# Both layers of a mixture-of-depths block as seven block products, in sections of one attention group

## The chip, the cores and the metric

The kernel runs on one core of a Trainium2 chip. The time is the device time of one execution in microseconds; three runs are shown, and the median counts. A core has five engines that run beside each other, each through its own list of instructions in order: TensorE (PE, with its weight loads as PEld), VectorE (DVE), ScalarE (ACT), GpSimd (POOL) and SyncE (SP, which issues most transfers). They wait for each other by semaphores.

## The reference

Attention with normalized queries and keys on 8 batches of 12 heads, 448 tokens and 64 values per head, then a layer that works on 128 chosen tokens of each batch:

```python
q_n, k_n = (rmsnorm(q, g_q), rmsnorm(k, g_k))          # (8, 12, 448, 64)
scores = scale * np.matmul(q_n, k_n.transpose(0, 1, 3, 2))
attn = softmax(scores)
x = np.matmul(attn, v)                                 # -> (8, 448, 768)
...
scores = np.einsum('bsd,d->bs', x, w_gate)
out = x.copy()
for b in range(B):
    top_idx = np.argpartition(-scores[b], capacity)[:capacity]   # capacity 128
    xe = x[b, top_idx]
    h = np.maximum(xe @ w1, 0.0)                       # w1 768 x 1024: layer 1
    ye = h @ w2                                        # w2 1024 x 768: layer 2
    g = 1.0 / (1.0 + np.exp(-scores[b, top_idx]))
    out[b, top_idx] = x[b, top_idx] + g[:, None] * ye
```

All is in float32.

## The kernel before, in words

**Attention.** The heads of a batch are three groups of four; 24 groups in all, numbered n. A group has seven units u (64 keys each, for four heads). `scores(u)` multiplies keys by queries into two PSUM banks of the pool `ps_sc` (four banks, handed out in turn) and has ScalarE take two exponentials into a tile `p` (seven of them). `values(u)` multiplies by v and collects a group in two banks of `ps_av`. `add_probs` adds the `p` tiles on VectorE; in the first six groups the last two units of a group are left to TensorE. When a group has ended, `values_out` copies its result out of PSUM on ScalarE (two copies), `sum_keys` makes the softmax sums (`den_ps`), `invert_sums` transposes them and takes the reciprocal on VectorE, and two calls of `to_tokens` transpose the result (four transposes each) and multiply it by the reciprocal on VectorE (x out of `x_ps`). `gate` multiplies by `w_gate` (four products on VectorE). For a whole batch follow `store_x`, `spread`, `score_rows` (four transposes and a copy), `count` (the rank of each token by comparisons on VectorE), `annotate`, `select` (four indirect DMAs on POOL that write the chosen rows to DRAM), and `load_selected` (SP loads them as `xe`).

**Preparing later groups** is laid in slots: `at(slot, fn)` runs `fn` when the loop has reached unit `slot`. The loads of tokens, q, k, v stand 11 to 26 units ahead, then `squares` (ScalarE), `sum_squares` (VectorE and POOL), `rows_out`, `rows_in` (through DRAM), `scale_q` (VectorE). The weights are loaded in 14 parts from slot 16 on, every third slot.

**The two layers** are in `mixture(g)`, a generator whose pieces the loop takes one at a time. The batches are grouped 0, 1-2, 3-4, 5-6, 7. For all of them layer 1 is the plain product: the weights are the stationary operand, and 128 tokens (a single batch) or 256 (a pair) are the moving one; ScalarE takes the maximum with 0 out of PSUM. Layer 2 of a single batch is plain too, 384 columns of w2 at a time. Layer 2 of a pair takes seven block products instead of eight: the hidden tiles are cut in a 2 x 2 block matrix (rows are the two batches, columns the halves of the hidden width), w2 in four blocks, and sums and differences of blocks (s1 to s4 on VectorE) are multiplied by w2 blocks or mixed blocks. The mixed blocks (`mix`, a subtraction on VectorE of 128 x 768 elements) are made once, stored to DRAM (`store_mixed`), and loaded again through a ring of two buffers (`load_mixed`). Four of the seven products add up in one bank, `main`; the others use a `side` bank of `ps_sc`. `gated` multiplies by the gate and adds to `xe` on VectorE; `write` puts the rows out by an indirect DMA.

**The loop** runs in sections of four units: scores of two, values of two, again, and after that up to two pieces of `mixture` and tasks from a list (`tasks`, `opening`), whose place is worked out while the program is made (`ready`, `pieces`, `long_next`, `single`). Batch 0's pieces start as soon as its chosen rows are there.

Of the kernel before, what the change touches and what calls it, by code (L numbers as in the profile page):

```python
# [68 lines left out]
def fast(  # L69
# [24 lines left out]
    CP = 112  # L94
# [30 lines left out]
    spare = [False]  # L125

    def aux(shape, name):

        if PER * now[0] >= units:
            return ps_sc.tile(shape, F32, tag="sc", name=name)  # L130
        if spare[0]:
            return ps_moe.tile(shape, F32, tag="moe", name=name)
        return ps_aux.tile(shape, F32, tag="aux", name=name)
# [38 lines left out]
    w1 = const.tile([128, NDC, F], F32, name="w1")  # L172
    HF, HD = NFC // 2, DM // 2
    w2 = {b: const.tile([128, HF, HD], F32, name=f"w2_{b[0]}{b[1]}") for b in ((0, 0), (1, 0), (1, 1))}
    mixed = [dram_pool.tile([128, HF, HD], F32, name=f"mixed{i}", bufs=1) for i in range(4)]
# [22 lines left out]
    def load_w(part):  # L198
        if part < NDC:
            nc.sync.dma_start(  # L200
                out=w1[:, part], in_=moe_w1.rearrange("(c p) f -> p c f", p=128)[:, part]
            )
            return
        k, part = divmod(part - NDC, 2)
        load_block(((0, 0), (1, 0), (0, 1), (1, 1))[k], part)

    def in_ring(what):
        ring[what] = moe_pool.tile([128, HF, HD], F32, name="ring", bufs=2)
        return ring[what]

    def chunk(part):
        return slice(HF // 2 * part, HF // 2 * (part + 1))

    def load_block(b, part):
        dst = w2[b] if b in w2 else ring["B12"] if part else in_ring("B12")
        src = moe_w2.rearrange("(k f p) (h c) -> k h p f c", p=128, f=HF, c=HD)[b[0], b[1]]
        nc.sync.dma_start(out=dst[:, chunk(part)], in_=src[:, chunk(part)])

    def load_mixed(i, part):
        dst = ring[i] if part else in_ring(i)  # L220
        nc.sync.dma_start(out=dst[:, chunk(part)], in_=mixed[i][:, chunk(part)])

    def store_mixed(i, part):
        nc.sync.dma_start(out=mixed[i][:, chunk(part)], in_=ring[i][:, chunk(part)])

    def mix(i, part):

        if part == 0:
            if i == 1:
                ring[1] = ring["B12"]  # L230
            else:
                in_ring(i)
        a, b = {
            1: (ring.get("B12"), w2[0, 0]),
            3: (w2[1, 1], ring.get("B12")),
            2: (w2[1, 1], ring.get(1)),
            0: (w2[1, 0], ring.get(2)),
        }[i]
        f = chunk(part)
        nc.vector.tensor_tensor(out=ring[i][:, f], in0=a[:, f], in1=b[:, f], op=OP.subtract)  # L240
# [104 lines left out]
    def values(u):  # L345
        n, i = divmod(u, NI)
        if i == 0:
            avs[n] = [ps_av.tile([128, 512], F32, name="av") for _ in range(2)]
        for hh in (1, 0):
            for c in range(2):  # L350
                r = slice(D * c, D * (c + 1))
                nc.tensor.matmul(  # L352
                    out=avs[n][c][D * hh : D * (hh + 1), 0:S],
                    lhsT=get("v", n)[r, hh, i, :],
                    rhs=probs[u][r, hh],
                    start=(i == 0),
                    stop=(i == NI - 1),
                )
# [13 lines left out]
    def values_out(n):  # L372
        for c in (1, 0):
# [11 lines left out]
    def sum_keys(n):  # L385

        add_late()
        ps = aux([128, 512], "den_ps")
# [16 lines left out]
        dens[n] = den  # L405
        if n < n_groups - 1:

            q, place = now
            when = (q, place + 1) if place == 0 or long_next(q) else (q + 1, 0)
            tasks.insert(0, (when, lambda: invert_sums(n)))  # L410

    def invert_sums(n):
        den = dens.pop(n)
        shape = [128, 128]
        if now[1] == 0 and PER * now[0] < units:
            pool, tag = (ps_moe, "moe") if before_layers(now[0]) else (ps_sc, "sc")
            ps = pool.tile(shape, F32, tag=tag, name="denT_ps")
        else:
            ps = aux(shape, "denT_ps")
        nc.tensor.transpose(out=ps[:CP, :], in_=den, identity=ident)  # L420
# [3 lines left out]
            in_=ps[:CP].rearrange("p (t r) -> p t r", r=32)[:, :, 0:NJ].rearrange(  # L424
# [5 lines left out]
    def to_tokens(n, c):  # L430
# [4 lines left out]
        shape = [128, NJ, 128]  # L435
        if c == 1 and not (before_layers(now[0]) or spare[0] or now[1] == 1 and single(now[0])):
            ps = ps_sc.tile(shape, F32, tag="sc", name="x_ps")
        else:
            ps = aux(shape, "x_ps")
# [8 lines left out]
        )  # L448

# [39 lines left out]
    def score_rows(b):  # L489
        if before_layers(now[0]):  # L490
            ps = aux([128, 512], "row_ps")
        else:

            ps = ps_sc.tile([128, 512], F32, tag="sc", name="row_ps")
# [65 lines left out]
    groups = [(0,)] + [(b, b + 1) for b in range(1, B - 2, 2)]  # L560
    groups += [(b,) for b in range(1 + 2 * (len(groups) - 1), B)]
    group_of = {b: g for g, bs in enumerate(groups) for b in bs}

    def mixture(g):

        n, bs = CAP, groups[g]
        G = len(bs)
        wide = 128 * G
        xe = [xes.pop(b) for b in bs]
        last = bs[-1] == B - 1  # L570
        xeT = moe_pool.tile([128, NDC, 2, 128], F32, name="xeT")
        hT = moe_pool.tile([128, NFC, 2, 128], F32, name="hT")

        def bank():

            if PER * now[0] >= units:
                return ps_sc.tile([128, 512], F32, tag="sc", name="sc")
            return ps_moe.tile([128, 512], F32, tag="moe", name="moe_ps")

        half = NDC // 2  # L580
        rows = []

        parts_out = ((0, HD), (DM - 2 * HD // 3, DM), (HD, DM - 2 * HD // 3)) if last else ((0, DM),)

        def write(i, k):
            c0, c1 = parts_out[k]
# [7 lines left out]
        def gated(i, cols, ps):  # L594
            x = xe[i]
            nc.vector.scalar_tensor_tensor(  # L596
                out=x[:n, cols],
                in0=ps[:n, : cols.stop - cols.start],
                scalar=x[:n, DM : DM + 1],
                in1=x[:n, cols],  # L600
# [3 lines left out]

        for i, x in enumerate(xe):
            for a in range(2):
                ps = ps_sc.tile([128, 512], F32, tag="sc", name="xeT_ps") if a else bank()
                for d in range(half):
                    dc = half * a + d
# [6 lines left out]
                    out=xeT[:, half * a : half * (a + 1), i, :n],  # L616
                    in_=ps[:, : half * 128].rearrange("p (i t) -> p i t", t=128)[:, :, :n],
                )
                if a == 1:
                    row = moe_pool.tile([128, len(parts_out)], I32, name="row", bufs=4)  # L620
                    for k, (c0, c1) in enumerate(parts_out):
                        nc.vector.tensor_scalar(
                            out=row[:n, k : k + 1],
                            in0=x[:n, DM + 1 : DM + 2],
                            scalar1=float(DM // (c1 - c0)),
# [863 lines left out]
```

## Time and profile before

| | |
|---|---|
| runs shown | 514.47, 518.47, 518.48 us, median 518.47 |
| the profiled execution | 513.42 us |
| its span, first to last instruction | 511.7 us |
| TensorE (PE) busy | 491.6 us, 96% |
| VectorE (DVE) busy | 354.0 us, 69% |
| ScalarE (ACT) busy | 274.8 us, 54% |
| GpSimd (POOL) busy | 187.0 us, 37% |
| layer 1, matmuls in the trace | 288 of 256 columns, 192 of 128 columns |
| layer 2, matmuls in the trace | 168 in products of pairs (384 columns), 64 for single batches |
| moved by DMA | 105.82 MB |

Times are measured from the start of the span. A matmul of float32 is two instructions in the trace. Of a group of instructions the busy time is that in which at least one of them ran; matmuls overlap, so their pace is read from start to start. L and a number is the line of the kernel.

### The profile page before, as it was taken

The page shows a single profiled execution, that of the slowest core. Times are in us where ns is not written, and L with a number is a line of the kernel's source. Part 1 is how long each engine was busy: PE and PEld are TensorE (multiplying, and loading weights), DVE is VectorE, ACT ScalarE, POOL GpSimd, SP SyncE. Part 2 cuts the span into 40 slices and gives each one's busy share as a digit, 9 for nine tenths or more (in the row PEclk, how much of TensorE's full clock was granted, in tenths as well). Part 3 has the DMA queues.
Part 4 walks back from the last instruction along what each step waited for, and adds up shares of the span by engine and source line. Part 5 has one row for each costly group of instructions (what it writes and reads, how often), then busy time and mean ns, then how long its engine had stood idle before and what let it go on. Part 6 is the DMA issues. An engine that isn't in the chain of part 4 may idle for free. (4 is left out here: it accounts for less than half of the span.)

```text
span 511.7 us, 11121 instructions
## 1 busy us (share of the span) xinstructions
PE 491.6 (96%) x4429; PEld 279.4 (55%) x4429; DVE 354.0 (69%) x670; ACT 274.8 (54%) x507; POOL 187.0 (37%) x104
## 2 busy tenths in 40 slices
PE   5999999988999999999999999999999899999994
PEld 4544445435555444666654454665554454786683
DVE  4566898699866898996687886777567686623201
ACT  4787886866757466665454737654634536310000
POOL 4694548444524174427123085036220022020102
PEclk9999999999999999999999999999999999999998
DMA  8977889999964673899461989567423318232601
GB/s 294 387 247 257 271 272 365 326 296 319 283 204 129 214 248 121 283 323 331 134 201 26 350 280 302 190 191 207 136 72 88 110 38 260 89 109 58 221 3 36
DMA packets 49295, 105.82 MB, mean 207 GB/s; under 512 B 11571, under 2 KB 26420, under 8 KB 49234
## 3 DMA queue, kind: packets, MB, share of 16 engines
q1 hardware_dynamic: 45826, 98.70, 59.9%
q0 software_dynamic: 3264, 6.31, 3.7%
q8 instruction: 37, 0.61, 0.5%
q14 instruction: 24, 0.20, 0.1%
q10 hardware_dynamic: 144, 0.00, 0.0%
HBM read 84.37 MB, written 28.50 MB: 221 GB/s over the span
## 5 line engine op out<-in xcount | busy, mean ns | idle before, releaser
L337 ACT ACTIVATE p<-sc,rinv 128x448 f32<-128x448 f32 x336 | 186.0, 641 | 88.3 <-PE sc L328 74.3
L256 POOL TENSOR_TENSOR rinv<-ss,neg_half 128x14 f32<-128x14 f32 (+1 forms) x49 | 135.7, 2775 | 184.4 <-DVE ss L255 164.9
L328 PE MATMUL sc<-qT,kT 64*64 64x448 f32 x1344 | 152.7, 545 | 1.0 <-DVE qT L307 0.8
L352 PE MATMUL av<-p,v 64*64 64x448 f32 x1344 | 147.0, 537 | 0.0
L368 DVE TENSOR_TENSOR sum<-sum,p 128x896 f32<-128x896 f32 x107 | 116.5, 1089 | 8.1 <-ACT p L337 1.9
L352 PEld LDWEIGHTS av<-p,v 64*64 64x64 f32 x1344 | 57.6, 133 | 69.6 <-issue 62.3
L328 PEld LDWEIGHTS sc<-qT,kT 64*64 64x64 f32 x1344 | 52.5, 132 | 69.3 <-issue 43.8
L255 DVE TENSOR_REDUCE ss<-sq 128x14 f32<-128x910 f32 (+1 forms) x49 | 52.1, 1074 | 11.9 <-ACT sq L246 11.6
L639 PE MATMUL moe_ps<-xeT,w 128*128 128x256 f32 (+1 forms) x288 | 56.1, 347 | 0.0
L539 POOL DMA_INDIRECT selected<-x,rank x32 | 35.8, 1118 | 47.7 <-DVE x L531 39.7
L639 PEld LDWEIGHTS moe_ps<-xeT,w 128*128 128x128 f32 x288 | 46.2, 191 | 6.8 <-issue 2.6
L246 ACT ACTIVATE sq<-tok 128x896 f32<-128x896 f32 (+1 forms) x49 | 45.9, 949 | 5.9 <-DMA tok<-in_tok_dram 5.6
L443 DVE TENSOR_TENSOR x<-x_ps,rden 112x512 f32<-112x512 f32 x48 | 32.5, 687 | 20.8 <-PE x_ps L441 18.3
L467 DVE SCALAR_TENSOR_TENSOR prod<-x,wg 112x256 f32<-112x256 f32 x96 | 40.6, 423 | 2.9
L587 POOL DMA_INDIRECT out_dram<-xe,row x10 | 10.5, 1052 | 85.7 <-DVE xe L596 67.9
L639 PE MATMUL sc<-xeT,w 128*128 128x256 f32 (+1 forms) x192 | 32.2, 328 | 0.3 <-ACT xeT L615 0.3
L441 PE MATMUL x_ps<-ident,xT 128*112 128x128 f32 x192 | 28.8, 276 | 2.0 <-DVE x L443 2.0
L639 PEld LDWEIGHTS sc<-xeT,w 128*128 128x128 f32 x192 | 28.8, 191 | 2.8 <-ACT xeT L615 0.5
L287 DVE SCALAR_TENSOR_TENSOR qT<-qT,gg,bc 128x896 f32<-128x896 f32 x22 | 25.3, 1149 | 4.4 <-DMA bc<-rows 4.4
L512 DVE SCALAR_TENSOR_TENSOR cmp<-score_rows,gate,earlier 112x448 f32<-112x448 f32 x32 | 21.9, 684 | 9.1 <-ACT score_rows L502 8.1
L441 PEld LDWEIGHTS x_ps<-ident,xT 128*112 128x112 f32 x192 | 21.8, 134 | 10.3 <-issue 4.5
L368 DVE TENSOR_TENSOR sum<-p 128x896 f32<-128x896 f32 x24 | 25.9, 1078 | 1.8 <-ACT p L337 1.8
(87 smaller groups left out, 331.9 us busy)
## 6 DMA issues: line engine op xcount, KB each, us to landing
tok<-in_tok_dram SPq DMA_DIRECT2D x48, 448.0 KB, 6.6
qT<-in_qT_dram SPq DMA_DIRECT2D x24, 448.0 KB, 6.6
kT<-in_kT_dram SPq DMA_DIRECT2D x24, 448.0 KB, 7.1
v<-in_vp_dram SPq DMA_DIRECT2D x24, 448.0 KB, 7.6
out_dram<-x SPq DMA_DIRECT2D x8, 1344.0 KB, 9.0
bc<-rows SPq DMA_DIRECT2D x44, 224.0 KB, 6.4
ring<-mixed SPq DMA_DIRECT2D x22, 384.0 KB, 5.3
xe<-selected SPq DMA_DIRECT2D x8, 385.0 KB, 3.7
```

Source lines behind the costliest of these rows:

```text
L246: nc.scalar.activation(out=sq[:, h, :, 0:D], in_=t[:, h], func=AF.Square, scale=scale)
L255: nc.vector.tensor_reduce(out=ss[:, h], in_=sq[:, h], axis=AX.X, op=OP.add)
L256: nc.gpsimd.tensor_tensor(out=rinv[:, h].rearrange(flat), in0=ss[:, h].rearrange(flat), in1=neg_half.to_broadcast([128, (h.stop - h.start) ...
L328: nc.tensor.matmul(out=scs[hh][D * c : D * (c + 1), 0:S], lhsT=get("kT", n)[r, c, D * i : D * (i + 1)], rhs=get("qT", n)[r, c, :], start=True,
L337: nc.scalar.activation(out=p[:, hh], in_=scs[hh][:, 0:S], func=AF.Exp, scale=rinvs[n, 1][:, hh, i : i + 1],)
L352: nc.tensor.matmul(out=avs[n][c][D * hh : D * (hh + 1), 0:S], lhsT=get("v", n)[r, hh, i, :], rhs=probs[u][r, hh], start=(i == 0), stop=(i ...
L368: nc.vector.tensor_tensor(out=sums[n], in0=probs.pop(u - 1) if begins else sums[n], in1=probs.pop(u), op=OP.add)
L441: nc.tensor.transpose(out=ps[:CP, j, :], in_=t[:, j, :], identity=ident)
L443: nc.vector.tensor_tensor(out=xs[b][:, :, col : col + 128].rearrange("p j (h d) -> p j h d", d=D), in0=ps[:CP].rearrange("p j (h d) -> p j ...
L467: nc.vector.scalar_tensor_tensor(out=prod[:, 0 : GH * D], in0=xs[b][:, j, cols], scalar=1.0, in1=wg[:, cols], op0=OP.mult, op1=OP.mult, ac ...
L539: w = nc.gpsimd.indirect_dma_start(out=t[:, :], out_offset=bass.IndirectOffsetOnAxis(ap=rank[:, j : j + 1], axis=0), in_=x[:, j, :], in_of ...
L639: nc.tensor.matmul(out=ps[:, i, :, :n], lhsT=w1[:, dc, 128 * (f0 + i) : 128 * (f0 + i + 1)], rhs=xeT[:, dc, 0:G, :n], start=(dc == 0), sto ...
```

## The change

The batches are taken in pairs 0-1, 2-3, 4-5, 6-7, and both layers use seven block products. In layer 1 the inputs (transposed tokens, `xeT`) are the 2 x 2 block matrix, w1 is in four blocks of 384 x 512, and a product is 12 matmuls of 128 columns. What a product gives belongs to one or two of the four hidden tiles (`share`): the first that comes is copied out of PSUM by ScalarE, a later one is added by VectorE, and after the last the maximum with 0 is taken on ScalarE. Four layer-1 blocks are mixed too, and the mixed blocks of both layers go through one ring of three buffers; each use of a block asks for the one that comes three uses later (`used`). The first pair makes the mixed blocks on the way, so its layer-1 order is 1, 2, 3, 6, 5, 7, 4, where later pairs have 1, 2, 6, 5, 7, 3, 4.

The sections now are one group (seven units), and the tasks stand in them at fixed places. The first eight groups (`FIRST = 8`) hold attention only, in two parts of four and three units. From group 8 on a section has its seven units, then `sum_keys`, a piece, `invert_sums`, first tokens, mostly a second piece, second tokens, sometimes a third piece. After the last group the rest of pair 4-5 and all of pair 6-7 follow. `load_selected` stands seven slots after the score rows (before ten), and the PSUM bank of each task is named in the call (`bank`).

The diff, cut to its core (an entry of `todo_products` tells whether the product goes to the main bank, its weight block, its input, and the hidden tiles that it belongs to; the second `if g == 0` is that of layer 2):

```diff
-    groups = [(0,)] + [(b, b + 1) for b in range(1, B - 2, 2)]
...
+    uses = [(l, i) for l in (1, 2) for i in (2, 1, 3, 0)]
+    to_load = uses * (B // 2 - 1)
...
+    def mix_all(l, i):
+        for part in range(2):
+            mix(l, i, part)
+            at(soon() + 3 + part, store_mixed, l, i, part)
...
-        ring[what] = moe_pool.tile([128, HF, HD], F32, name="ring", bufs=2)
+        ring[what] = moe_pool.tile([128, BLOCK], F32, name="ring", bufs=3)
...
     def invert_sums(n):
-        den = dens.pop(n)
...
+        den, ps = dens.pop(n)
+        ps = ps[:CP, 128:256]
         nc.tensor.transpose(out=ps, in_=den, identity=ident)
...
+        def used(l, i):
+            if not to_load or g == 0 and (l == 1 or i == 2):
+                return
+            what = to_load.pop(0)
+            s = soon()
+            for part in range(2):
+                at(s + 4 + 2 * part if s >= 0 else s, load_mixed, *what, part)
...
-        chunks = 4 // G
-        for f0 in range(0, NFC, chunks):
...
-                        lhsT=w1[:, dc, 128 * (f0 + i) : 128 * (f0 + i + 1)],
-                        rhs=xeT[:, dc, 0:G, :n],
...
+        def product(ps, w, h, first):
+            for f in range(HF):
+                for d in range(HC):
+                    nc.tensor.matmul(
+                        out=ps[:, 128 * f : 128 * f + n],
+                        lhsT=w[:, d, 128 * f : 128 * (f + 1)],
+                        rhs=h[:, d, :n],
...
+        def share(k, ps, begun):
...
+            if not begun:
+                nc.scalar.activation(out=h[:, :, :n], in_=ps, func=AF.Relu if last_one else AF.Copy)
+                return
+            nc.vector.tensor_tensor(out=h[:, :, :n], in0=h[:, :, :n], in1=ps, op=OP.add)
+            if last_one:
+                nc.scalar.activation(out=h[:, :, :n], in_=h[:, :, :n], func=AF.Relu)
...
+        todo_products = {
+            1: (True, (0, 0), lambda: a11, (1,)),
+            2: (False, (1, 0), lambda: a12, (1,)),
+            6: (True, 2, lambda: s2, (2,)),
+            5: (False, 1, lambda: s1, (2, 4)),
+            7: (True, 3, lambda: s3, (4,)),
+            3: (False, (1, 1), lambda: s4, (2,)),
+            4: (True, 0, lambda: a22, (3,)),
+        }
+        for k in (1, 2, 3, 6, 5, 7, 4) if g == 0 else (1, 2, 6, 5, 7, 3, 4):
...
+            if g == 0:
+                if k == 5:
+                    mix_all(1, 0)
+                if k == 7:
+                    for part in range(2):
+                        load_block(2, (0, 1), part)
             yield
...
+            if g == 0:
+                if k == 1:
+                    mix_all(2, 3)
+                    mix_all(2, 1)
+                if k == 2:
+                    mix_all(2, 2)
+                if k == 5:
+                    mix_all(2, 0)
...
-        at(s + 10 if s >= 0 else s + 3, load_selected, b)
+        at(s + 7 if s >= 0 else s, load_selected, b)
...
+    for k, i in enumerate((3, 1, 2)):
+        for part in range(2):
+            at(NI * FIRST + 2 * k + part, mix, 1, i, part)
+            at(NI * FIRST + 2 * k + part + 3, store_mixed, 1, i, part)
...
+    for q in range(n_groups):
+        u0 = NI * q
...
+        for i in range(0, NI, 2):
+            for u in (i, i + 1):
+                if u < NI:
+                    scores(u0 + u)
+            run_values(u0 + i - 1 if i < NI - 1 else u0 + i - 2)
+        slot[0] = u0
+        sum_keys(q - 1)
+        if q == FIRST:
+            to_tokens(q - 2, 1, ps_sc)
+        if g == 1 and b > 2:
+            ranks_of(b - 1)
+        run(u0 + 1)
+        next(moe)
+        slot[0] = u0 + 2
+        invert_sums(q - 1)
+        to_tokens(q - 1, 0, ps_sc)
+        run(u0 + 3)
+        if q not in (21, 23):
+            next(moe)
+        slot[0] = u0 + 4
+        to_tokens(q - 1, 1, ps_aux)
+        run(u0 + 6)
+        if q not in (10, 11, 13, 15, 17, 19) and q < 20:
+            next(moe)
+        run(u0 + 6)
```

## The prediction

> **What bounds the kernel now.** I read the engine table first, then the stretches, then TensorE's own order in time and its waits. The engine table and the busy tenths:
>
> ```profile
> PE 491.6 (96%) x4429; PEld 279.4 (55%) x4429; DVE 354.0 (69%) x670; ACT 274.8 (54%) x507; POOL 187.0 (37%) x104
> ...
> PE   5999999988999999999999999999999899999994
> ...
> DVE  4566898699866898996687886777567686623201
> ```
>
> TensorE is busy nearly everywhere, VectorE 69% on average, but with tenths of 8 and 9 in the first half. The table of stretches (busy us of PE, PEld, DVE, ACT, POOL, then clock and DMA share) shows how close VectorE comes:
>
> ```profile
> 64.00:96.00 32.00, 32.00 (x382) 15.47 (x374) 28.32 (x56) 25.08 (x47) 20.06 (x10) 1.00 0.95 329
> 96.00:128.00 32.00, 28.59 (x325) 15.05 (x321) 27.56 (x57) 20.47 (x39) 12.82 (x8) 1.00 1.02 302
> ...
> 208.00:224.00 16.00, 16.00 (x134) 9.38 (x130) 15.38 (x27) 8.79 (x18) 8.29 (x2) 1.00 0.84 282
> ```
>
> From 208 to 224 us, where the weight blocks are mixed, VectorE is 96% busy and TensorE does not stop: there it has just enough cover. From 96 to 128 us it hasn't. Busy time doesn't say at which rate TensorE works; its order in time does (start, length, count):
>
> ```profile
> 449.90 13.13 PE L639 MATMUL sc<-xeT,w 128*128 128x256 f32 x60
> 462.86 2.74 PE L683 MATMUL moe_ps<-w,hT 128*128 128x384 f32 x8
> 465.44 2.74 PE L683 MATMUL side_ps<-w,hT 128*128 128x384 f32 x8
> ...
> 483.01 10.98 PE L639 MATMUL sc<-xeT,w 128*128 128x128 f32 x96 [0.29 <-ACT xeT L615]
> 493.83 5.33 PE L659 MATMUL sc<-w,hT 128*128 128x384 f32 x16
> ```
>
> From start to start: 256 columns 12.96/60 = 0.216 us, 384 columns 2.58/8 = 0.3225, 128 columns 10.82/96 = 0.1127. So cost goes by columns, 4% dearer at 128, and there is no idle time between. TensorE's waits:
>
> ```profile
> PE den_ps L396 <- DVE x L443: 2.6, 4, 1.4
> PE x_ps L441 <- DVE x L443: 2.0, 2, 1.6
> PE den_ps L396 <- DVE row L622: 1.2, 1, 1.2
> ```
>
> All three are VectorE late in its own order: small, but of the kind that the change multiplies.
>
> **What it removes.** Each matmul of the program is two in the trace. Layer 1 now: 288 of 256 columns and 192 of 128, 288 x 0.216 + 192 x 0.1127 = 83.8 us. After: 4 pairs x 7 products x 12 matmuls x 2 = 672 of 128 columns, 75.7 us: -8.1. Layer 2 now: 168 in products and 64 for the two single batches (one half split into 256 and 128 columns, nearly the same), 232 x 0.3225 = 74.8; after 4 x 28 x 2 = 224, 72.2: -2.6. All of it lies on TensorE's path: **-10.7**. The three waits above (5.8) hang on the old places of tasks, so I take them off: **-5.8**. Attention, its sums and transposes keep their counts. Base: 511.7 - 16.5 = 495.2 us of span.
>
> [...] The 96 matmuls above had a new weight load each and ran at 0.1127 against 0.3225 for 384, so the row decides.
>
> **What it adds on VectorE.** Per pair four differences of layer-1 inputs (0.5 us each, between 0.61 for 512 elements and nothing) and four additions of a PSUM block to the hidden tile (nearest row: L443 from PSUM, 0.65); eight more mixes (L240, 0.87 from start to start); one pair more of layer-2 differences. About 20 + 7 + 3 = 30 us on 354, and they stand in one queue with the work that frees TensorE's banks. So I walk the sections in the order in which the changed program issues its instructions (a section is one group of heads, its seven units first), with costs from start to start: reciprocal 0.25, x out of PSUM 0.65, sum of squares 1.0, the four gate products 1.75, q scaling 1.1, one mix 0.87, a count 0.73, a gated addition 0.55. TensorE: a layer-1 product 2.7, a layer-2 product 2.6, four token transposes 0.45, a unit's scores 0.75.
>
> Group 8 (first with blocks). Between the first tokens and the reciprocal VectorE has x, mix, gate, scaling, mix, rows = 5.4; TensorE has 12 input transposes 1.35, 0.16, 0.45, product one 2.7 = 4.7, and its second tokens need the bank that the reciprocal reads: wait 0.7. Then VectorE's order up to the addition that frees product two's bank: 0.25 + 0.65 + 1.0 + 2 mixes 1.74 + three differences 1.45 + 0.65 + 1.0 + 0.87 + 1.75 + 0.87 + 0.65 = 10.9. TensorE meanwhile: 0.45 + 2.7 + one unit of scores 0.75 = 3.9, and the second unit's scores take just that bank, the fourth in the ring of four. Wait **7.0** at the start of group 9. Queued behind: all scores, so all of ScalarE.
> Group 10: its second scores wait 1.3 for group 9's last addition in the same way. Then product 7 and product 4 stand in the same bank without another between (only the first pair has that order), and the addition between them is behind counts and scaling: VectorE 6.2 us after attention's end, TensorE 4.2: 2.0.
> Group 11: behind layer 2's first product gated 0.55, differences 1.85, four mixes 3.5, reciprocal 0.25 = 6.15, against 0.16 + 0.45 + 2.6: 2.9; then 1.0 at the next scores. Groups 14 and 17 end on a side product with gate work ahead of its release: 0.6 each.
> Sum 0.7 + 7.0 + 1.3 + 2.0 + 2.9 + 1.0 + 1.2 = **+16.1**. The bounds: nothing, if the queue is ahead as at 208-224, and 20, if the rows' full durations count instead of start to start.
>
> [...] This trace only shows transposes at 108.04 waiting 1.64 us for VectorE, one instance.
>
> **Waits on transfers.** From a batch's score rows to the issue of its chosen rows' load the trace has 15.5 to 19.3 us in mid kernel (340.6 to 356.1, 114.0 to 133.3), and 3.7 to landing (median). The changed order asks for them some 18.6 us after the score rows in groups 14 and 20: 0.6 to 4.4 late; I take 1.5 each, **+3** (0 to 9).
> At the end SP's queue has batch 7's chosen rows ahead of the last pair-three block. That load waits for the selection: score rows at 449.5, issue at 461.1, 11.6 us. Only then go two block loads, 0.8 to issue and 4 to 5 to land, so the block is there 17 us after the score rows. TensorE has five layer-2 products, 13.3. **+4** (0 to 6). The six products also cover batch 7's own rows (15.3).
> Attention in one block of seven units with four score banks: ScalarE has 14 exponentials of 0.64 and two copies of 0.55 = 10.1 in TensorE's 10.6. The chain in a block gives 0 to 0.4 of wait; sixteen blocks, **+2** (0 to 6). Transfers grow by 26 block loads and 8 stores more, 13 MB, in stretches where the DMA share is 0.5 to 0.8: nothing.
>
> Sum: 495.2 + 16.1 + 3 + 4 + 2 = 520.3 us of span, +8.6. The profiled execution took 513.42 us, its span 511.7; the runs shown have 514.47 to 518.48, median 518.47. I put the difference on the median: 527.1, say **527**.
>
> **Rivals.**
> A, faster: the removed columns come through because VectorE is always ahead. For it: 208 to 224, 15.38 of 16 busy and no stop. Against: those mixes had a section of other work between them. 495.2 + 4 + 2 + 1 = 502.2: -9.5, 509 us. It decides if the wait at group 9's start is under 2 us.
> B, no change: only the bank that the next scores need holds TensorE (7.0 + 1.0); the rest is absorbed. 495.2 + 8 + 1.5 + 4 + 2 = 510.7: 517.5 us.
> C, slower still, by transfers: the first eight groups now hold attention alone, at 12.6 to 13.6 us of TensorE each, and the DMA share at 64 to 128 us is 0.95 to 1.02 already. A group there brings five loads of 448 KB, two of 224, some 2.3 weight parts of 430 and a third of a 1344 KB store, 4.2 MB; at the 302 GB/s of 96 to 128 us that is 13.9 us. Up to 1 us for each of five groups: 525 of span, 532 us. Against: the loads are asked for 11 to 26 units (of 1.5 us) ahead.
> D, the change saves nothing because weight loads bind at 128 columns: 672 x (0.191 - 0.1127) = 53 us more, if a load took its profiled mean of 0.191 each. The 96 matmuls at 483.01 speak against it; under 0.02.
>
> **How the numbers follow.** Forecast 0.49 (520 to 533 us), A 0.18, B 0.24, C 0.08, D 0.01. A measurement of this kernel can tell about 1% from no change. A is faster, B the same, the others slower: 0.18, 0.24, 0.58. The range takes in most of A at its low end and the forecast's upper bounds (VectorE 20, rows 9, attention 6): 509 to 538.
>
> **What would show it.** Layer-1 matmuls at 0.11 us from start to start and 75.7 us in sum: right for the first step. TensorE waiting for VectorE's addition into the hidden tile at the scores of group 9 for 5 us or more, and at the second tokens of group 11 for 2 to 3: right for the third. A dense tail but for some 4 us before the last product of pair three. Wrong if all TensorE waits on VectorE stay under 6 us in sum, or if group 8's first scores, now at 128.0 us, come after 124 (worked out: 11.5 + 8 x 13.4 = 119).

## The result, and the profile after

The change made the kernel slower: 552.64 us median (549.26 to 553.58, four runs) against 516.65 for the kernel before on the same chip, a ratio of 1.069, 95% interval 1.063 to 1.076. The forecast was 527, slower, in a range of 509 to 538: the sign was right, the size was not. The profiled execution took 549.26 us with a span of 547.5; its work is compared below with the span of 511.7 before.

The engine table of the profile after, the busy tenths of TensorE and the clock that it was granted in the same 40 slices:

```profile
PE 492.2 (90%) x4605; PEld 295.7 (54%) x4605; DVE 381.1 (70%) x718; ACT 284.5 (52%) x519; POOL 189.7 (35%) x104
...
PE   5979999989959889799979999999979999939990
...
PEclk9998999999979899999999999999999999978997
```

TensorE's busy time is what it was (492.2 against 491.6), though its work is less; its share fell from 96 to 90%. In the third line digits of 7 and 8 are new, at slices 4, 12, 14, 36 and 37. The kernel before had full clock up to its end:

```profile
PEclk9999999999999999999999999999999999999998
```

TensorE's order in time (start, length, count), two products of layer 1 and two of layer 2 at the end:

```profile
508.36 2.84 PE L643 MATMUL moe_ps<-xeT,ring 128*128 128x128 f32 x24
511.04 2.84 PE L643 MATMUL side_ps<-xeT,w 128*128 128x128 f32 x24
...
521.56 2.74 PE L705 MATMUL moe_ps<-ring,xeT 128*128 128x384 f32 x8
524.14 2.74 PE L705 MATMUL side_ps<-ring,xeT 128*128 128x384 f32 x8
```

From start to start 2.68 us for 24 matmuls of 128 columns (0.112 each) and 2.58 for 8 of 384. So the products are as cheap as forecast, and the loss stands between them. TensorE's waits (what it waited for, us in all, times, longest):

```profile
PE moe_ps L705 <- DMA ring<-mixed: 8.4, 1, 8.4
PE xeT_ps L611 <- DMA xe<-selected: 6.5, 3, 3.2
PE sc L337 <- DVE hT L660: 5.8, 1, 5.8
PE x_ps L435 <- DVE rden L420: 5.1, 4, 3.1
...
PE moe_ps L643 <- DVE hT L660: 1.8, 1, 1.8
PE sc L337 <- ACT hT L658: 1.6, 1, 1.6
```

Without the one at the start, all such waits made 7.8 us in the kernel before; now they make 38. The stretches around three of them (busy us of PE, PEld, DVE, ACT, POOL, then the clock, the DMA share, GB/s):

```profile
144.00:160.00 16.00, 9.51 (x77) 7.56 (x79) 15.65 (x36) 3.32 (x7) 7.79 (x2) 0.92 0.92 318
160.00:176.00 16.00, 16.00 (x151) 9.30 (x144) 7.68 (x9) 10.51 (x20) 0.00 (x0) 0.86 0.58 162
...
480.00:496.00 16.00, 7.62 (x18) 3.77 (x17) 1.24 (x2) 0.00 (x0) 1.89 (x2) 0.68 0.58 197
```

From 144 to 160 VectorE works 15.65 of 16 us while TensorE stands; from 160 to 176 TensorE has no wait, and yet a clock of 0.86. The clock records of this trace say 0.5 at 41.5 to 44.9, 157.6 to 164.4, 184.9 to 188.3 and 485.3 to 495.5 us, each beginning inside a stop of TensorE or at most 0.4 us behind one.

To add it up I price each run of equal matmuls at its closest pace (0.111 us for 128 columns, 0.323 for 384, and so on), and call what it took beyond that excess. Paced work: 462.6 us before, 450.7 after, **-11.9**. Excess: 36.7 before, 79.4 after, **+42.7**. From the start of the last run of TensorE to the end of the span: 8.4 before, 13.1 after, **+4.7**. The sum is +35.5, against +35.8 in the spans.

### The profile page after: what moved, and what is told of

Same layout as the page of the kernel before. It is cut to its first block, busy times and chain, and to the rows that moved or that the text cites. A ratio compares the mean times of both kernels' runs of the same rounds, so it can differ in the third digit from the quotient of the medians.

```text
span 547.5 us, 11644 instructions
## 1 busy us (share of the span) xinstructions
PE 492.2 (90%) x4605; PEld 295.7 (54%) x4605; DVE 381.1 (70%) x718; ACT 284.5 (52%) x519; POOL 189.7 (35%) x104
## 5 line engine op out<-in xcount | busy, mean ns | idle before, releaser
L346 ACT ACTIVATE p<-sc,rinv 128x448 f32<-128x448 f32 x336 | 188.3, 640 | 92.7 <-issue 48.3
L337 PE MATMUL sc<-qT,kT 64*64 64x448 f32 x1344 | 171.9, 553 | 14.5 <-DVE hT L660 5.8
L361 PE MATMUL av<-p,v 64*64 64x448 f32 x1344 | 165.5, 548 | 0.4 <-ACT xT L384 0.3
L337 PEld LDWEIGHTS sc<-qT,kT 64*64 64x64 f32 x1344 | 61.8, 134 | 85.3 <-issue 43.7
L361 PEld LDWEIGHTS av<-p,v 64*64 64x64 f32 x1344 | 68.2, 136 | 65.9 <-issue 54.5
L531 POOL DMA_INDIRECT selected<-x,rank x32 | 39.7, 1240 | 68.6 <-DVE x L523 60.4
L578 DVE SCALAR_TENSOR_TENSOR xe<-moe_ps,xe 128x384 f32<-128x384 f32 (+2 forms) x17 | 10.0, 590 | 32.9 <-PE moe_ps L705 32.9
L662 ACT ACTIVATE hT<-hT 128x512 f32<-128x512 f32 x12 | 7.6, 630 | 46.5 <-DVE hT L660 46.5
L384 ACT COPY xT<-av 128x448 f32<-128x448 f32 x48 | 23.4, 539 | 10.1 <-PE av L361 6.9
L643 PE MATMUL moe_ps<-xeT,ring 128*128 128x128 f32 x192 | 23.1, 277 | 1.8 <-DVE hT L660 1.8
```

What stands on the lines that cost most here:

```text
L337: nc.tensor.matmul(out=scs[hh][D * c : D * (c + 1), 0:S], lhsT=get("kT", n)[r, c, D * i : D * (i + 1)], rhs=get("qT", n)[r, c, :], start=True,
L346: nc.scalar.activation(out=p[:, hh], in_=scs[hh][:, 0:S], func=AF.Exp, scale=rinvs[n, 1][:, hh, i : i + 1],)
L361: nc.tensor.matmul(out=avs[n][c][D * hh : D * (hh + 1), 0:S], lhsT=get("v", n)[r, hh, i, :], rhs=probs[u][r, hh], start=(i == 0), stop=(i ...
L531: w = nc.gpsimd.indirect_dma_start(out=t[:, :], out_offset=bass.IndirectOffsetOnAxis(ap=rank[:, j : j + 1], axis=0), in_=x[:, j, :], in_of ...
```

## The experiments

All but the control start from the changed kernel. The ratio is always to the kernel before, timed beside it on the same chip; the changed kernel itself stands at 1.069.

| run | what | ratio, 95% interval |
|---|---|---|
| e2_fourth | fourth buffer for chosen rows | 1.058 (1.052 to 1.063) |
| e1_both | and the ring block ahead of the rows | 1.047 (1.043 to 1.051) |
| e3_mixes | layer 1's mixes early | 1.062 (1.057 to 1.066) |
| e4_select | chosen rows written a slot earlier | 1.066 (1.057 to 1.075) |
| e5_add | additions ahead in groups 8, 9 | 1.040 (1.032 to 1.048) |
| e6_fill | idle time filled with transposes | 1.063 (1.051 to 1.076) |
| e7_qt | q scaling of group 2 early | 1.064 (1.056 to 1.071) |
| e8_all | all orders mended | 1.006 (1.002 to 1.009) |
| e9_end | last rows in one piece | 1.061 (1.056 to 1.067) |
| e10_best | orders mended again, with e9 | 0.984 (0.980 to 0.988) |
| e11_before_end | kernel before, last rows in one piece | 1.000 (0.997 to 1.003) |
| e12_pool | as e10, mixes on GpSimd | 0.995 (0.993 to 0.998) |

**The tail: e2_fourth.** TensorE stops at 483.2, behind the next to last product of pair three, for 8.4 us. SyncE's queue there, in the changed kernel:

```profile
467.64 0.61 SPq L451 DMA_DIRECT2D out_dram<-x  x1
487.37 0.32 SPq L549 DMA_DIRECT2D xe<-selected  x1
487.81 37.33 SPq L221 DMA_DIRECT2D ring<-mixed  x18
```

The ring block goes out 0.4 us behind batch 7's chosen rows. My forecast had those wait for the selection, whose last write POOL issues at 479.96. POOL's order shows another candidate, batch 4's rows on their way out, 3.2 us before SyncE moves on:

```profile
484.17 0.98 POOL L569 DMA_INDIRECT out_dram<-xe,row  x1 [3.26 <-DVE xe L578]
```

There are three buffers `xe`, so batch 7 takes batch 4's.

```diff
-            xs[b] = x_pool.tile([CP, NJ, DX], F32, name="x")
+            xs[b] = x_pool.tile([128, NJ, DX], F32, name="x")[:CP]
...
-        xe = moe_pool.tile([128, DX], F32, name="xe", bufs=3)
+        if b < B - 1:
+            xe = moe_pool.tile([128, DX], F32, name="xe", bufs=3)
+        else:
+            xe = x_pool.tile([128, NJ, DX], F32, name="x")[:, 0]
```

> The last batch's chosen rows go into a fourth buffer instead of the third (a token tile that is free by then); nothing else changes. In the changed kernel SyncE issues them at 487.37 us, 6.5 us after the last selection write was issued, and the ring block that TensorE waits for is behind them. Theory 1 (the buffer): the load waits because its buffer still holds batch 4's rows, whose write to the output went out at 484.17, one product before. Then with a fourth buffer the load is issued some 1.8 us after the selection (as in the kernel before), at about 482.7, the ring block lands near 487, the wait of 8.4 us before the last product of pair three becomes 3.5 to 4.5, and the time falls by 4 to 7 us (the smaller wait should also leave less of the half clock behind it). Theory 2 (my prediction's: the selection itself is late): the load stays at 487 and nothing changes, within 1 us.

SyncE issues the rows at 482.38 and the ring block at 482.82, and of TensorE's 8.4 us there are left:

```profile
PE moe_ps L708 <- DMA ring<-mixed: 3.8, 1, 3.8
```

Theory 1: the buffer made the rest. The 3.8 that stay are the wait that my forecast had worked out (4). The time falls by about 1.2% of the kernel before, some 6 us.

**The tail: e1_both.** The rows are asked for behind the ring block as well.

```diff
-        at(s + 7 if s >= 0 else s, load_selected, b)
+        if b < B - 1:
+            at(s + 7, load_selected, b)
...
-    for _ in moe:
+    for i, _ in enumerate(moe):
         run(units)
+        if i == 1:
+            load_selected(B - 1)
```

> The fourth buffer as above, and the last batch's chosen rows are asked for after the ring block of pair three's last product instead of before it. Theory 1 (the tail's loss is SyncE's order and the buffer, and nothing else): no wait before the last product of pair three, none over 1 us before pair four's transposes, the clock stays at 1.00 from 480 to 500 us, and the time falls by 9 to 11 us against the changed kernel. Theory 2 (transfers are too slow in the tail whatever their order): the wait moves to the transposes of pair four, at 4 us or more, and the time falls by less than 6.

As theory 1 had it: no wait at the last product, 0.2 us at pair four's transposes, clock 1.00 from 403 to 526 us. 2.2% of 515.5 is 11.6 us less than the changed kernel. Transfers in the tail are fast enough once they are in order.

**Group 9: e3_mixes and e5_add.** Where TensorE stops at 153.5 VectorE works without a break. Its order in time (start, length; the lines of the gate products but the first are left out) up to the addition into the hidden tile, line 660, that frees the bank of group 9's scores:

```profile
155.04 0.94 DVE L244 TENSOR_TENSOR ring<-w,ring 128x768 f32<-128x768 f32 x1
155.91 0.43 DVE L463 SCALAR_TENSOR_TENSOR prod<-x,wg 112x256 f32<-112x256 f32 x1
...
157.67 0.95 DVE L244 TENSOR_TENSOR ring<-w,ring 128x768 f32<-128x768 f32 x1
158.54 0.68 DVE L660 TENSOR_TENSOR hT<-hT,side_ps 128x512 f32<-128x512 f32 x1
```

```diff
 e3_mixes: in the loop over k, i in enumerate((3, 1, 2)) and part
-            at(NI * FIRST + 2 * k + part, mix, 1, i, part)
-            at(NI * FIRST + 2 * k + part + 3, store_mixed, 1, i, part)
+            early = NI * (FIRST - 3) + 4 + 2 * (2 * k + part)
+            at(early, mix, 1, i, part)
+            at(early + 3, store_mixed, 1, i, part)
```

> The six mixes of layer 1's blocks are moved from group 8 to groups 5 to 7, every second slot; group 8 and all after it keep their other work. Theory 1 (VectorE's one queue: the mixes stand ahead of the addition that frees the bank of group 9's scores): that wait of 5.8 us falls to 1 to 3, the 0.9 us before group 8's second product goes, the half clock at 157.6 to 164.4 goes, and the time falls by 6 to 9 us if groups 5 to 7 have room on VectorE, by 2 to 5 if they have not (then group 7 starts later by the difference). Theory 2 (the section of seven units itself, with a product on the bank that the next scores take, is what costs): the wait stays above 4.5 us, and the time falls by less than 2.

The wait at group 9 fell to 1.45 us and the one before group 8's second product went, but group 7's first scores now wait 3.6 us for VectorE instead of 1.8, which is 15.62 of 16 us busy from 112 to 128, and half clock follows there (a mean of 0.89 over these 16 us). So the mixes do stand in the way, theory 1, and groups 5 to 7 have no room for them: some 4 us, its second figure.

```diff
 e5_add:
-        run(u0 + 6)
+        if q not in (8, 9):
+            run(u0 + 6)
         if q not in (10, 11, 13, 15, 17, 19) and q < 20:
             next(moe)
         run(u0 + 6)
```

> In groups 8 and 9 the section's third product, and with it the addition that frees its bank, is issued ahead of the last slots' work (sum of squares, mixes, four gate products, scaling) instead of behind it; no work is added or removed. Theory 1 (the place of the addition in VectorE's one queue makes the wait): the wait of 5.8 us at the first scores of group 9 falls to 1.5 or less, that of 1.6 at group 10 goes, and with them the half clock behind each (157.6 to 164.4 and 184.9 to 188.3 in the changed kernel): 8 to 11 us less. Theory 2 (VectorE simply has too much to do in groups 8 and 9, so what is passed over is late at the next bank): as much wait comes back inside groups 9 to 11, and the time falls by less than 4 us.

In its trace, VectorE's order in time, the addition starts 5.0 us behind the start of product two (148.4), not 9.5 as in the changed kernel (149.0 and 158.54):

```profile
153.47 0.68 DVE L660 TENSOR_TENSOR hT<-hT,side_ps 128x512 f32<-128x512 f32 x1
```

The wait is 1.29 us, that at group 10 is down to 0.28, and nothing there has half clock behind it: group 10 starts at 173.87 instead of 181.47. Nothing of it comes back in groups 9 to 11. Theory 1; the profiled span is 8.0 us shorter, the ratio 2.9% lower, with intervals of nearly 1% on each side. (The profiled execution is the slowest of e5_add's four, and that of the changed kernel the fastest of its own.) The same work in another order, no more.

**The clock: e6_fill.**

```diff
+        if q == 9:
+            ps = bank(ps_aux, name="fill_ps")
+            for _ in range(36):
+                nc.tensor.transpose(out=ps[:, 0:128], in_=ident, identity=ident)
         for i in range(0, NI, 2):
```

> 36 transposes of the identity matrix into the bank of the second tokens (free some 2.3 us after TensorE stops) are put ahead of group 9's scores: 4 us of useless TensorE work inside the 5.8 us in which it waits for VectorE; all else is unchanged. Theory 1 (the half clock of 157.6 to 164.4 us follows from TensorE standing idle): the first scores still start when the addition is done, at about the same time, but the clock stays at 1.00 through the following 8 us and TensorE's work there is 2.5 to 3.5 us shorter; the time falls by 1 to 4 us although work was added. Theory 2 (the clock falls for another reason, or the wait is all that costs): the half clock stays, and the time is the same or up to 1 us longer.

In between. The transposes begin at 154.26, behind 2.33 us of idle time, and the clock falls all the same, for 3.4 us at 154.5 instead of 6.8 at 157.6: it falls on the filling work, which takes 5.82 us (an estimate of 36 transposes at the 0.112 us of a 128-column matmul here is 4.0). From the start of product two (149.0 and 149.1) the scores behind the stop come 0.7 us later than in the changed kernel (where ten matmuls of scores run ahead of it, here none); but what follows runs at full clock (1.00 from 160 to 176 us where it was 0.86), and group 10 starts 1.1 us earlier in spite of that. So here too the half clock came behind a stop of TensorE, one of 2.33 us where the changed kernel had 5.79. The times show no difference (1.063 with an interval of over 1% on each side).

**Group 2: e7_qt.**

```diff
-            at(max(s0 - 6, first + 11), scale_q, n)
+            at(max(s0 - 6, first + (10 if n == 2 else 11)), scale_q, n)
```

> The q scaling of group 2 is issued one section part earlier on VectorE, ahead of the reciprocal that waits for the den sums of group 0, instead of behind the reciprocal and the first tokens. Theory 1 (group 2's scores wait only for that place in the queue): the 3.0 us before them go, the half clock at 41.5 to 45 goes, and the time falls by 3 to 5 us. Theory 2 (the broadcast rows that the scaling reads have not landed any earlier): the scaling waits for them, and the time falls by less than 1 us.

On the spot theory 1: the stop of 2.9 us in front of group 2's scores and its half clock are gone, and the values at 66.2, counted from the first scores, come 4.6 us earlier. In the span nothing is to be seen of it, and the ratio, 0.5% lower, is within the noise, so the gain in time is not shown: this execution has half clock at 111.7, 224.3, 278.9 and 398.4, behind stops of 1.8 to 3.2 us that in the profiled execution of the changed kernel had none. The same stop had half clock behind it in this execution and not in that one. The executions of the changed kernel show it too: spans of 547.5 and 548.8 us at mean clocks of 0.971 and 0.968, of 550.8 to 553.5 at 0.957 to 0.959.

**Chosen rows: e4_select.**

```diff
-        at(s + 2 if s >= 0 else s, annotate, b)
-        at(s + 2 if s >= 0 else s, select, b)
+        at(s + 1 if s >= 0 else s, annotate, b)
+        at(s + 1 if s >= 0 else s, select, b)
```

> The rank and the writes of the chosen rows are issued one slot earlier, ahead of the section's first product, reciprocal and normalisation, in all batches. Theory 1 (in groups 14 and 20 the rows come late because the selection stands on GpSimd behind a power of 2.6 us and on VectorE behind the sum of squares): the chosen rows are issued 3 to 5 us earlier, the two waits of 3.3 and 3.4 us before the transposes of pairs two and three fall under 1 us each, and the time falls by 4 to 7 us. Theory 2 (my prediction's: the slot in which SyncE is asked for the rows sets it): the slot of that load is unchanged, so the waits stay within 0.5 us and so does the time.

GpSimd's first write for pair two is issued at 265.35 instead of 270.93, and both waits of pairs two and three are gone. That speaks for theory 1: the selection was late, not the slot of the load. But the time hardly moves. TensorE stands 1.97 and 1.91 us in groups 13 and 19, in front of the values, and 0.7 us more in group 10. The profile names ScalarE's copy out of `av`; that copy in turn waits for TensorE, whose values for it had ended at 269.6. The semaphore updates that tell of it are recorded only from 272.44 on, seven within 0.3 us. What held them is not settled; e8_all has two such stops, in groups 10 and 13, of 2.2 and 2.3 us. In e10_best, where these two batches have their writes first in the slot, as in e8_all, there is none.

**All orders together: e8_all.** With the edits of e1_both, e3_mixes, e5_add and e7_qt there are three more:

```diff
         if b < 2 or s < 0:
             ...                              # annotate and select as before
+        else:
+            todo.setdefault(s + 2, []).insert(0, lambda: (annotate(b), select(b)))
...
-        for k in (1, 2, 3, 6, 5, 7, 4) if g == 0 else (1, 2, 6, 5, 7, 3, 4):
+        for k in (1, 2, 6, 5, 7, 3, 4):
...
-                    mix_all(2, 3)
-                    mix_all(2, 1)
+                    at(soon(), mix_all, 2, 3)
+                    at(soon(), mix_all, 2, 1)
```

> All orders mended together, with the same products, mixes and transfers: the two tail edits, the early mixes, the addition ahead of other work in groups 8 and 9, q scaling of group 2 early, the chosen rows' writes first in their slot (batches 2 to 7) and so ahead of GpSimd's power, pair one's layer-1 products in the order of the other pairs (product 3 between 7 and 4), and the mixes of layer 2 behind group 11's reciprocal. Theory 1 (the loss is made of a few places in the queues and the half clock behind each): the parts sum to 10.5 tail, 11 at groups 9 and 10, 4 at group 2, 6 at the chosen rows, 2 and 3 at groups 10 and 11, some 37 us, so the span is about 511 and the time 508 to 520, the same as before the change. Theory 2 (seven block products in these sections cost more in themselves, by weight loads, transfers or VectorE's extra 27 us): the time stays above 528.

519.53 us, 0.6% above the kernel before (interval 0.2 to 0.9): theory 1. The products, mixes and transfers are those of the changed kernel, and 33 us are gone. The waits inside groups 10 (1.8) and 11 (3.1) are not in its list any more.

**The end: e9_end and the control e11_before_end.** In the changed kernel the rows of the last pair go out in four writes, here on POOL:

```profile
532.97 0.96 POOL L569 DMA_INDIRECT out_dram<-xe,row  x1 [34.60 <-DVE xe L578]
536.90 0.96 POOL L569 DMA_INDIRECT out_dram<-xe,row  x1 [2.96 <-DMA out_dram<-xe,row]
540.64 0.96 POOL L569 DMA_INDIRECT out_dram<-xe,row  x1 [2.78 <-issue]
543.81 0.96 POOL L569 DMA_INDIRECT out_dram<-xe,row  x1 [2.21 <-issue]
```

The last values are ready at 535.9 (a gated addition of 0.35 from 535.54), 8 us before the write that carries them.

```diff
-        last = bs[-1] == B - 1
+        last = False
```

> The last batch's output rows are written in one piece behind the last product instead of in three, and the last product is not split; nothing else changes. In the changed kernel the last TensorE instruction starts at 535.2 and the span ends at 547.5, 12.3 us later, against some 7 in the kernel before (504.2 and 511.7). Theory 1 (a term that my sum lacked: four writes of the last pair, each waiting for the one before, some 3.7 us apart from 532.97 on): with two writes the second goes out at about 536.9, the span ends near 540.5, and the time falls by 6 to 8 us. Theory 2 (the end after the last product is as long as before and the writes overlap, as my sum took it): the time rises by up to 1 us, since the last piece is larger.

> Control: the kernel before the change, with its last batch's output rows written in one piece behind the last product instead of three. There the three writes went out at 500.51, 504.15 and 507.96 and the last product started to end at 504.2. Theory 1 (each write waits for the one before): the one write goes out at about 505.2 and the span ends near 509, 2 to 3 us less. Theory 2 (the writes overlap the last product): the same or up to 1 us more. It also gives the fair measure for the mended kernel: what is left between the two is the change itself.

e9: the writes go out at 535.25 and 541.49 and the span ends 10.7 us behind the first of them instead of 14.5: **3.8** us less, about what the ratio shows (0.8%), not 6 to 8. The chain is there as theory 1 has it, but a write of whole rows holds the next back for 6.2 us, not 3.7. In the kernel before the same edit leaves the time as it was, 1.000, as theory 2 says. Its profiled execution is 2.2 us late before the end begins (a write that went out at 483.00 goes at 485.23, behind a stop of 2.2 us at 106.4 and half clock). Set against that, the one write, at 507.90 instead of 507.96 for the last of three, goes out 2.2 us earlier, near where theory 1 had it, but the span ends 4.9 us behind it instead of 3.8. A chain of three so costs some 1 us here, less than the times can show, and a chain of four 3.8.

**Mended, and better than both: e10_best.** The edits of e1_both, e5_add, e7_qt and e9_end and the three of e8_all, with `if b not in (3, 5)` in the first of these; layer 1's mixes stay in group 8.

> The orders mended together, again with the same products and mixes, and with the last rows in one piece; the mixes of layer 1 stay in group 8 (moved early they cost a wait of 3.6 us at group 7), and only batches 3 and 5 write their chosen rows first in the slot. Theory 1 (only places in queues are left): 519.5 less 6.5 for the end and 2 to 4 for group 7, so 508 to 512 us, 1 to 1.5% under the kernel before: then the columns that the change saved are seen at last. Theory 2 (VectorE's 27 us of extra work cannot be hidden in groups 7 to 11 in any order, and only moves about): above 514 us, no better than the kernel before.

504.74 us against 513.01, 1.6% under the kernel before (interval 1.2 to 2.0): theory 1, and slightly more than the 1 to 1.5% expected. The control says that the end's edit alone gives the kernel before nothing, so the same 1.6% are left between the two with that edit. Of its profile, the engine table, the clock and the largest waits behind the start:

```profile
PE 477.8 (95%) x4597; PEld 286.2 (57%) x4597; DVE 380.2 (76%) x715; ACT 282.9 (56%) x519; POOL 185.0 (37%) x102
...
PEclk9999999999999999999999999999999999999997
```

```profile
PE sc L337 <- DVE x L437: 1.8, 1, 1.8
PE den_ps L404 <- DVE sum L377: 1.8, 2, 0.9
PE sc L337 <- DVE hT L663: 1.3, 1, 1.3
```

No stop of TensorE is over 1.9 us, and the clock is full up to the end of its work. Paced work 450.7, excess 36.5: the work of the changed kernel with the excess of the one before. Its span is 502.8, 8.9 us under 511.7. So VectorE's extra 27 us can be hidden, and theory 2 falls.

**Mixes on GpSimd: e12_pool.**

```diff
-        nc.vector.tensor_tensor(out=ring[l, i][:, f], ...)
+        engine = nc.gpsimd if l == 1 and i != 0 else nc.vector
+        engine.tensor_tensor(out=ring[l, i][:, f], ...)
```

> As the mended kernel with the last rows in one piece, and layer 1's first six mixes are computed by GpSimd instead of VectorE, from group 5 on (every second slot). Theory 1 (VectorE is full from group 5 to 9, 14.8 to 15.4 us busy in each 16, and its fullness is what is left of the loss there): the waits on VectorE at groups 7 and 9 fall, and the time is 2 to 5 us below that of the mended kernel. Theory 2 (GpSimd takes so long for a mix that its powers for the next groups come late): the time is the same or up to 8 us more, with ScalarE or VectorE waiting for the power.

510.73 us, 6 more than e10_best, whose other edits it has, with the early mixes of e3_mixes. The time is that of theory 2; its mechanism is not. A mix takes GpSimd 2.4 us (VectorE 0.95), and it is busy 13.74 of 16 us from 112 to 128. But the power that comes late (112.19, in e10_best 107.61) has GpSimd idle for 2.9 us before it, waiting for VectorE. What the mixes slow is VectorE beside them. GpSimd's mixes, three of VectorE's gate products, and the scores that TensorE then starts:

```profile
102.56 4.78 POOL L245 TENSOR_TENSOR ring<-w,ring 128x768 f32<-128x768 f32 x2
107.30 1.99 POOL L245 TENSOR_TENSOR ring<-ring,w 128x768 f32<-128x768 f32 x1
...
105.71 1.92 DVE L464 SCALAR_TENSOR_TENSOR prod<-x,wg 112x256 f32<-112x256 f32 x1
107.67 1.90 DVE L464 SCALAR_TENSOR_TENSOR prod<-x,wg 112x256 f32<-112x256 f32 x1
109.61 0.43 DVE L464 SCALAR_TENSOR_TENSOR prod<-x,wg 112x256 f32<-112x256 f32 x1
...
111.20 3.22 PE L338 MATMUL sc<-qT,kT 64*64 64x448 f32 x10 [3.42 <-issue]
```

Beside a mix a gate product took 1.9 us and more, behind the last one 0.43 again. The q scaling stands behind them on VectorE and ends at 111.11; the scores that read it begin at 111.20, after a stop of 3.4 us for which the profile names no releaser, and the clock is 0.5 from 110.4 to 120.6. The wait of 1.3 us at group 9 is gone, as theory 1 had it, and one of 2.8 for chosen rows is new at 143.7. How much of the 6 us is the other engine and how much the early place is not separated: no run has the early mixes on VectorE with the other edits of e10_best.

## Why the prediction was right in part, and where it failed

**Right: the columns.** -10.7 forecast, 11.9 less paced work measured. The changed kernel takes 0.112 us a matmul at 128 columns and 0.322 at 384, close to the 0.1127 and 0.3225 that the forecast was priced with.

**Right: VectorE's queue in the sections.** The excess of each place, forecast first: second tokens of group 8, 0.7 and 0.9; start of group 9, 7.0 and 6.3; start of group 10, 1.3 and 2.2; product 7 to 4, 2.0 and 2.0; group 11, 2.9 and 3.3; start of group 12, 1.0 and 0.6; groups 14 and 17, 1.2 and nothing. Together 16.1 and 15.3; the sum is nearer than its parts, as group 10 and groups 14 and 17 nearly cancel. At the start of group 10 the path also has a step that the forecast lacks: the bank's last reader is a copy on ScalarE (184.20), in line behind the maximum that waits for VectorE's addition (182.95). That the addition's place in the order sets its release is what e5_add shows: with the same work in another order the wait at group 9 was 1.29 us, where the changed kernel has 5.8.

**Failed: a stop was priced at its own length.** The sum added waits and went on at full pace. Each of the four half-clock stages made the work behind it dearer: 1.7, 2.8, 1.8 and 2.1 us beyond its pace, **8.4** in all, a term that is nowhere in the prediction. The trace of before could not show it: its longest stops were 1.2 to 1.6 us, and its clock was full. A larger wait than any in the trace is outside what the trace prices.

**Failed: the tail, +4 with a bound of 6, measured 8.4.** The step "that load waits for the selection" named one condition of the load. The buffer, handed out three batches before, was the later one; e2_fourth took it away, and 3.8 were left. In the forecast's bound the buffer should have stood beside the selection.

**Failed: the end.** The span minus TensorE's work was taken over from before. The last group is a pair instead of one batch, so four writes stand in a chain instead of three: +4.7, of which e9_end gave 3.8 back.

**Mis-sized: the chosen rows, +3, measured 6.7** (3.3 and 3.4; bounds 0 to 9). The prediction set them by the slot of the load; the selection behind GpSimd's power set them, as e4_select shows (in the changed kernel pair two's ranks were ready at 268.7, the power ran from 268.12 to 270.74, the first write went out at 270.93).

**Missed: the first eight groups.** Group 8's first scores came at 130.4, past the 124 that I had set as a sign of error, not at 119. Part of it is the q scaling of group 2 (2.9 and the clock behind it, see e7_qt). Part is waits on VectorE at group 7, which I had taken off with the old places of tasks: 2.4 and 1.3. And 13.4 us a section was too little; e10_best, with hardly a stop in groups 0 to 6, needs some 13.8 and has group 8 at 124.6.

Half clock 8.4, tail 4.4, end 4.7, rows 3.7, group 2 2.9 and group 7 3.7 make 27.8; columns and sections came out 2.0 better. That is some 26 of the 27 us between the forecast span of 520.3 and 547.5. The range was also narrower than its own bounds: VectorE 20, rows 9 and attention 6 add to 541, not to its 538, and the half clock and the end lie outside them all.

The rivals. B fails with the waits of groups 8, 10 and 11, which were not absorbed. C had 532 and laid the loss on transfers in the first eight groups; no wait of TensorE there names a transfer. D, weight loads, is excluded by the 2.68 us above. A's condition, VectorE always ahead, did not hold in the changed kernel: the wait at group 9 was 5.8 us, not under 2. In e10_best it was nearly made true by hand (1.3 there), the tail and the end mended too, and A's 9.5 us under the kernel before are close to the 8.3 measured.

## What to carry to other kernels

When work is added to an engine that is off the bound, write its queue out in order and look for what frees a bank: the place of that one instruction in two groups decided 8 us of the span here, with the same work. Ask of every queued transfer for all that it waits for, its buffer too. And price a stop of TensorE with what may come behind it: in the changed kernel four of the ten stops of more than 1 us behind the start had 3.4 to 10.2 us at half clock behind them.

## What the runs showed of the hardware

**Half clock behind short stops.** The clock records of the changed kernel have four stages at 0.5 before the program's end, of 3.41, 6.83, 3.41 and 10.24 us, behind stops of TensorE of 2.89, 5.79, 1.65 and 8.38 us. Behind the six other stops of more than 1 us in that trace (1.18, 1.84, 1.84, 3.15, 3.06 and 3.20 us, the start left out) there was none, nor behind those of the kernel before (1.64, 1.22 and 1.40). Of the other runs, e6_fill had half clock behind a stop of 2.33 us, e12_pool behind 3.4 and e3_mixes behind 3.6. So 1.65 us had it here and 3.20 had not: the length of a stop alone does not tell. Nor does its place in the program: the stop of 3.15 us at 224.48 in the changed kernel had none, and one of the same length at 213.79 in e5_add had. What decides between them these runs do not show; a stop of 2 us is a risk already.

**VectorE beside GpSimd.** In e12_pool gate products took 1.9 to 2.0 us beside a GpSimd mix instead of 0.42, additions of `p` tiles up to 2.7 instead of 1.09. Beside GpSimd's powers they took their usual time: in the changed kernel 0.424 us a gate product and 1.089 an addition while a power ran, 0.425 and 1.091 without.

**Output writes in a chain.** They follow each other 3.2 to 3.9 us apart in the changed kernel's end, and 6.2 with whole rows in e9_end, while GpSimd itself is busy 0.96 us for each. The program orders them so: the second, at 536.90, waits for the semaphore of the first, which came at 536.21. The four writes of `select`, which the kernel declares independent of each other, go out 1.25 us apart (476.22 to 479.96). No run here declares the output writes independent.
